# Packing the last 96 gate and up columns of two chunks: one shared full-width tile per chunk and two column tiles

## The chip, the cores and the metric

The kernel runs on one core of a Trainium2 chip. The metric is the device time of one execution in microseconds, median over several runs. Nearly all runs are fast, with a granted TensorE clock of 0.999 to 1.000. PE is TensorE, PEld its weight loads, ACT ScalarE, DVE VectorE, POOL GpSimd.

## The reference, cut to what matters

The input `x` has 2048 rows of 512. It is layer normalised, and the result `xn` feeds a complex diagonal recurrence (with an input and an output projection) and a gated feed-forward block. The output is the sum of both and `x`.

```python
def _B_ref(x, w_gate, w_up, w_down):       # S, D, F = 2048, 512, 1376
    g = _silu(x @ w_gate)
    u = x @ w_up
    return (g * u) @ w_down

xn = _layernorm(x, axis=-1)
return x + _A_ref(xn, ...) + _B_ref(xn, B_w_gate, B_w_up, B_w_down)
```

What matters is that 1376 = 10 x 128 + 96: the gate and up matrices have ten full tiles of 128 columns and one of 96.

## The kernel before

The rows are worked in four chunks of 512. A chunk's transposed, normalised rows are `xnT[:, c % 2]`, so two chunks are on the chip at a time. A gate or up tile is four matmuls (512 input features in four steps) that stream 512 rows each into one PSUM bank. Tiles go in pairs, a pair of banks at a time, and the kernel takes four pairs of banks in turn; ScalarE evicts a pair, and VectorE multiplies gate and up. The eleventh tile stands alone.

```python
FP = [(0, 2), (2, 2), (4, 2), (6, 2), (8, 2), (10, 1)]      # (first tile, number of tiles)

def ffn_mm(c, i, which, bk):
    fs = fsz[i]                                              # 128, or 96 for the last tile
    ...
        for kt in range(KT):                                 # KT = 4
            inst = e.matmul(pbank[0:fs, bk, :]..., lhsT=w[:, kt, i * 128:i * 128 + fs], rhs=xnT[:, c % 2, :, kt, :],
                            start=(kt == 0), stop=(kt == KT - 1))

def ffn_up(c, ip):
    i0, n = FP[ip]
    bk = next_pair()
    for k in range(n):
        ffn_mm(c, i0 + k, "u", bk + k)
    rows = slice(0, 128 if n == 2 else fsz[i0])
    ...
    g.add("act", ... activation(out=uf[rows, ul, 0:n, :]..., in_=pair_f32(rows, bk, 512 * n), func=AF.Identity) ...)
    g.add("dve", ... tensor_tensor(out=hT[rows, hb, i0:i0 + n, :], in0=sg[rows, sl, 0:n, :], in1=uf[rows, ul, 0:n, :], op=ALU.mult) ...)
```

`ffn_gate` is the same with Silu. The order of the stages, which is the order of PE's queue:

```python
for ip in range(3, 6): ffn_gate(0, ip)
for ip in range(3, 6): ffn_up(0, ip)
u0 = ssm_b_chunk(0)                    # input projection of the recurrence
...
ln_chunk(2); xt_chunk_dma(2)           # layer norm of chunk 2, its transpose by DMA
...
u1 = ssm_b_chunk(1)
for ip in range(6): ffn_gate(1, ip); ffn_up(1, ip)
u2 = ssm_b_chunk(2)
...
dc_chunk(0)                            # down and output matrices of chunk 0
...
```

The queues of ScalarE, VectorE and GpSimd are ordered by a list scheduler with estimated durations; PE and the main DMA queue keep the order in which the program names the work.

Of the kernel before, what the change touches and what calls it, by code (L numbers as in the profile page):

```python
# [10 lines left out]
ALU = alu_op_type.AluOpType  # L11
F32 = mybir.dt.float32
B16 = mybir.dt.bfloat16
I32 = mybir.dt.int32
AF = mybir.ActivationFunctionType
# [223 lines left out]
def bass_parallel_sum__ssm_conv_s5__swiglu_ffn__prompt_kernel(  # L239
# [17 lines left out]
    Fh = B_w_gate.shape[1]  # L257
# [5 lines left out]
    KT = D // 128  # L263
    PT = P // 128
    FT = (Fh + 127) // 128
    fsz = [min(128, Fh - i * 128) for i in range(FT)]
# [3 lines left out]
    g = _Graph()  # L270
    es = ExitStack()
    with es:
        block = es.enter_context(nc.Block())

        def sb(name, shape, dt):
            return es.enter_context(nc.sbuf_tensor(name, shape, dt))
# [8 lines left out]
        NXN = 12  # L285
        xn_sb = sb("xn_sb", [128, NXN, D], B16)
        xnT = sb("xnT", [128, 2, 4, KT, 128], B16)
        wg = sb("wg", [128, KT, Fh], B16)
        wu = sb("wu", [128, KT, Fh], B16)
        wd = sb("wd", [128, FT, D], B16)  # L290
        BT = sb("BT", [128, 2, KT, P], B16)
# [1 line left out]
        hT = sb("hT", [128, 2, FT, CH], B16)  # L293
# [32 lines left out]
        NG = 4  # L326
        sg = sb("sg", [128, NG, 2, CH], B16)
        NUF = 2
        uf = sb("uf", [128, NUF, 2, CH], B16)
# [8 lines left out]
        pbank = _PB()  # L338
# [10 lines left out]
        def _bank_live(b):  # L349
            lw = g.last_w.get(("bk", b, 0))  # L350
            rd = g.readers.get(("bk", b, 0), ())
            return lw is not None and lw.eng == "pe" and len(rd) == 0 and not lw.name.startswith("pe_warm")

        def next_pair():
            for _ in range(NB // 2):
                b = 2 * (pair_ctr[0] % (NB // 2))
                pair_ctr[0] += 1
                if not (b in reserved or _bank_live(b) or _bank_live(b + 1)):
                    return b
            raise AssertionError("all PSUM pairs live")  # L360

        def pair_f32(rows, b, n=1024):
            return pb16[rows, b:b + 2, :].rearrange("p a f -> p (a f)").bitcast(F32)[:, 0:n]

        def BK(b):
            return [("bk", b, 0), ("bk", b, 1)]
# [55 lines left out]
        def loads_stage_b2():  # L422
# [12 lines left out]
              reads=[("ones",)], writes=[("ident",)], name="ident", est=300)  # L435
        g.add("pool", lambda e: e.iota(iot[:], pattern=[[1, TP]], base=0, channel_multiplier=0, allow_small_or_imprecise_dtypes=True),
              writes=[("iot",)], name="iota", est=1000)
# [4 lines left out]
              name="act_warm", est=220, order=(act_q[-1],))  # L442
# [22 lines left out]
        def bn_st(a, order=()):  # L465
            return g.add("dve", lambda e, a=a: e.bn_stats(out=st[:, a, :], in_=x_sb[:, a, :]),  # L466
                         reads=[("x", a)], writes=[("st", a)], name="bnst%d" % a, est=640, order=order)

        def bn_ag(a, order=()):
            return g.add("dve", lambda e, a=a: e.bn_aggr(out=mv[:, a, :], in_=st[:, a, :]),  # L470
                         reads=[("st", a)], writes=[("mv", a)], name="bnag%d" % a, est=90, order=order)

        def ln_ve(a, n, eng="dve", order=()):
            return g.add(eng, lambda e: e.tensor_scalar(out=ve[:, a:a + n], in0=mv[:, a:a + n, 1], scalar1=EPS, scalar2=None, op0=ALU.add),  # L474
                         reads=[("mv", a + j) for j in range(n)], writes=[("ve", a + j) for j in range(n)], name="ve%d" % a, est=70 if eng == "dve" else 230, order=order)

        def ln_rstd(a, n):
            return g.add("pool", lambda e: e.tensor_tensor(out=rstd[:, a:a + n], in0=ve[:, a:a + n], in1=mhalf[:, a:a + n], op=ALU.pow),  # L478
                         reads=[("ve", a + j) for j in range(n)] + [("mhalf",)], writes=[("rstd", a + j) for j in range(n)], name="rstd%d" % a, est=370 + 190 * n)
# [11 lines left out]
        def ln_apply_act(a0):  # L491
            g.add("dve", lambda e, a0=a0: e.scalar_tensor_tensor(out=nmr[:, a0:a0 + 4], in0=mv[:, a0:a0 + 4, 0], scalar=-1.0, in1=rstd[:, a0:a0 + 4], op0=ALU.mult, op1=ALU.mult),  # L492
                  reads=[("mv", a0 + j) for j in range(4)] + [("rstd", a0 + j) for j in range(4)], writes=[("nmr", a0 + j) for j in range(4)], name="nmr%d" % a0, est=70)
            for a in range(a0, a0 + 4):
                g.add("act", lambda e, a=a: e.activation(out=xn_sb[:, a % NXN, :], in_=x_sb[:, a, :], func=AF.Identity, scale=rstd[:, a:a + 1], bias=nmr[:, a:a + 1]),  # L495
                      reads=[("x", a), ("rstd", a), ("nmr", a)], writes=[("xn", a % NXN)], name="xn%d" % a, est=710)
# [22 lines left out]
        def ln_chunk(c):  # L519
            for a in range(4 * c, 4 * c + 4):  # L520
                bn_st(a)
                bn_ag(a)
            ln_ve(4 * c, 4, eng="pool")
            ln_rstd(4 * c, 4)
            if _CFG["ln_norm_act"][c]:
                ln_apply_act(4 * c)
            else:
                for a in range(4 * c, 4 * c + 4):
                    ln_apply(a)
# [23 lines left out]
        def xt_chunk_dma(c):  # L553
            s0 = (4 * c) % NXN
            dma("xTd%d" % c, xnT[:, c % 2].rearrange("p j k t -> p (j k) t"), xn_sb[:, s0:s0 + 4, :],
                [("xnT", c % 2, j) for j in range(4)], 4 * TILEB, reads=[("xn", s0 + j) for j in range(4)], xpose=True, prio=_CFG["prio_xt"])
# [136 lines left out]
        gctr = [0]  # L693
        uctr_f = [0]
# [4 lines left out]
                return [("wg", "a0"), ("wg", "a1")]  # L699
            return [(nm, 0 if i < 6 else 1)]  # L700

        FP = [(0, 2), (2, 2), (4, 2), (6, 2), (8, 2), (10, 1)]

        def ffn_mm(c, i, which, bk):
            fs = fsz[i]
# [9 lines left out]

        def silu_pair(c, ip, bk):
            i0, n = FP[ip]
            rows = slice(0, 128 if n == 2 else fsz[i0])
            sl = gctr[0] % NG
            gctr[0] += 1  # L720
            sg_slot[(c, ip)] = sl
            g.add("act", lambda e: e.activation(out=sg[rows, sl, 0:n, :].rearrange("p a t -> p (a t)"), in_=pair_f32(rows, bk, 512 * n), func=AF.Silu),  # L722
                  reads=sum([BK(bk + k) for k in range(n)], []), writes=[("sg", sl)], name="silu%d_%d" % (c, ip), est=63 + 427 * n)

        def ffn_gate(c, ip):
# [3 lines that stand above are left out]
                ffn_mm(c, i0 + k, "g", bk + k)  # L729
            silu_pair(c, ip, bk)  # L730
# [27 lines left out]
        def ffn_up(c, ip):  # L758
            i0, n = FP[ip]
            hb = c % 2  # L760
            bk = next_pair()
            for k in range(n):
                ffn_mm(c, i0 + k, "u", bk + k)
            rows = slice(0, 128 if n == 2 else fsz[i0])
            ul = uctr_f[0] % NUF
            uctr_f[0] += 1
            sl = sg_slot[(c, ip)]
            g.add("act", lambda e: e.activation(out=uf[rows, ul, 0:n, :].rearrange("p a t -> p (a t)"), in_=pair_f32(rows, bk, 512 * n), func=AF.Identity),  # L768
                  reads=sum([BK(bk + k) for k in range(n)], []), writes=[("uf", ul)], name="uev%d_%d" % (c, ip), est=63 + 427 * n)
            g.add("dve", lambda e: e.tensor_tensor(out=hT[rows, hb, i0:i0 + n, :], in0=sg[rows, sl, 0:n, :], in1=uf[rows, ul, 0:n, :], op=ALU.mult),  # L770
                  reads=[("sg", sl), ("uf", ul)], writes=[("hT", hb, i0 + k) for k in range(n)], name="hmul%d_%d" % (c, ip), est=77 + 267 * n)

        usctr = [0]
        uctr = [0]
# [17 lines left out]
        def ssm_b_chunk(c):  # L792
            return [ssm_b_unit(c, pt) for pt in range(PT)]
# [100 lines left out]
        loads_stage_b2()  # L894
        for ip in range(0, 3):
            ffn_up(0, ip)
        for ip in range(3, 6):
            ffn_gate(0, ip)
        for ip in range(3, 6):
            ffn_up(0, ip)  # L900
        u0 = ssm_b_chunk(0)
        ssm_elem_chunk(0, u0)
        ln_chunk(2)
        xt_chunk_dma(2)
        for pt in range(PT):
            wprep_C(pt)
        u1 = ssm_b_chunk(1)
        for ip in range(6):
            ffn_gate(1, ip)
            ffn_up(1, ip)  # L910
        u2 = ssm_b_chunk(2)
# [3 lines left out]
        resid_chunk(1)  # L915
        ln_chunk(3)
        xt_chunk_dma(3)
        for ip in range(6):
            ffn_gate(2, ip)
            ffn_up(2, ip)  # L920
        u3 = ssm_b_chunk(3)
        dc_chunk(1)
        ssm_elem_chunk(2, u2)
        ssm_elem_chunk(3, u3)
        for ip in range(6):
            ffn_gate(3, ip)
            ffn_up(3, ip)
        resid_chunk(2)
# [63 lines left out]
```

## Time and profile before

| | before |
|---|---|
| time, median of the first six runs | 181.66 us (181.49 to 182.05) |
| span of the profiled run | 180.3 us |
| PE, DVE, ACT busy | 97%, 89%, 47% |
| unbroken run of matmuls, from 13.63 us to 177.80 us | 164.17 us |
| the eleventh tiles | 32 matmuls |

First the busy line of the page, then pieces of the chain of waits (start, length, what).

```profile
PE 175.3 (97%) x900; PEld 84.9 (47%) x908; DVE 160.8 (89%) x274; ACT 84.5 (47%) x107; POOL 13.5 (7%) x23
```

```profile
13.63 13.81 PE pb L710 x64
27.44 13.81 PE pb L781 x64
41.26 18.99 PE pb L710 x88
60.25 6.91 PE pb L781 x32
...
175.01 2.79 PE pb L876 x20
```

L710 is the gate/up line, L781 the input projection of the recurrence, L876 the output matrices. From 13.63 us on the chain is PE work end to end. 64 matmuls take 13.81 us, and the 88 of one chunk's gate and up tiles 18.99 us: 215.8 ns each. I call 216 ns a slot. The groups by form (operation, tiles, weight shape, moving shape, count, then busy us, mean ns, and idle time before) show the eleventh tile on each engine:

```profile
L710 PE MATMUL pb<-xnT,wg 128*96 128x512 bf16 x16 | 4.1, 379 | 0.0
L710 PE MATMUL pb<-xnT,wu 128*96 128x512 bf16 x16 | 4.1, 379 | 0.0
L768 ACT ACTIVATE uf<-pb 96x512 bf16<-96x512 f32 x4 | 2.4, 590 | 0.4 <-DVE rot L812 0.4
L722 ACT ACTIVATE sg<-pb 96x512 bf16<-96x512 f32 x4 | 2.3, 586 | 0.0
L770 DVE TENSOR_TENSOR hT<-sg,uf 96x512 bf16<-96x512 bf16 x4 | 1.7, 413 | 0.0
```

A narrow tile is not cheaper: in the timeline of PE the two 96-wide tiles of chunk 1 begin 0.87 us apart, which is four slots.

```profile
58.36 1.03 PE L710 MATMUL pb<-xnT,wg 128*96 128x512 bf16 x4
59.23 1.03 PE L710 MATMUL pb<-xnT,wu 128*96 128x512 bf16 x4
```

The 379 ns are the recorded duration of one matmul, with a modelled end; the next starts 216 ns after it and overlaps the remaining 163 ns. What counts is start to start.

### The profile page before, as it was taken

The numbers are of one execution on the slowest core, as the hardware profiler recorded it, in microseconds if no ns is written. First come the engines' busy times: TensorE is split into PE (matmuls) and PEld (weight loads), VectorE is DVE, ScalarE is ACT, GpSimd is POOL, SyncE is SP. The second block draws the span as 40 slices with busy tenths as digits, with TensorE's granted clock in tenths as the row PEclk, the third lists the DMA queues.
The fourth block names the chain that finished last, engine by engine and source line by source line (L and its number), as shares of the span: only waits on it lengthen the run. The fifth ranks groups of instructions, "written<-read, shape, count | busy, mean of one in ns | idle before, by whom it ended". The sixth has DMA issues, their size and how long they took to land.

```text
span 180.3 us, 2342 instructions
## 1 busy us (share of the span) xinstructions
PE 175.3 (97%) x900; PEld 84.9 (47%) x908; DVE 160.8 (89%) x274; ACT 84.5 (47%) x107; POOL 13.5 (7%) x23
## 2 busy tenths in 40 slices
PE   8799999999999999999999999999999999999994
PEld 2494444444444444444444544444444444444643
DVE  3888849989799999979999999999999999999733
ACT  3279899995897991060655653000455620000000
POOL 3251200004200000320000000000000000000000
PEclk9999999999999999999999999999999999999999
DMA  6995556669160000001430000001200000000202
GB/s 163 316 373 127 119 100 104 149 201 343 33 116 0 4 0 0 0 0 61 91 86 0 0 0 4 0 0 36 80 0 4 0 0 0 0 0 33 87 29 87
DMA packets 23410, 12.37 MB, mean 69 GB/s; under 512 B 15112, under 2 KB 23400, under 8 KB 23400
## 3 DMA queue, kind: packets, MB, share of 16 engines
q1 hardware_dynamic: 22832, 11.70, 24.4%
q10 hardware_dynamic: 568, 0.53, 1.0%
q8 instruction: 7, 0.11, 0.3%
q14 instruction: 3, 0.02, 0.0%
HBM read 6.46 MB, written 2.10 MB: 47 GB/s over the span
## 4 chain that ended last, share of the span: by engine, by line
PE 94%; DMA 1%; DVE 1%; issue 1%; ACT 1%; POOL 0%
PE pb L710 39%; PE pb L863 21%; PE pb L781 15%; PE pb L876 15%; PE pb L749 3%; DMA x_sb<-in_A_x_dram 1%; ACT xnT L549 1%; PE pb L543 1%; DVE st L466 0%; POOL rstd L478 0%; DVE x_sb L881 0%; DVE xn_sb L485 0%; DVE mv L470 0%; DVE ve L474 0%; PE pb L457 0%
## 5 line engine op out<-in xcount | busy, mean ns | idle before, releaser
L710 PE MATMUL pb<-xnT,wu 128*128 128x512 bf16 (+1 forms) x176 | 41.2, 379 | 0.0
L821 DVE TENSOR_TENSOR_SCAN rot<-sm,car,rot 128x512 bf16<-128x512 f32 x32 | 38.9, 1267 | 0.0
L863 PE MATMUL pb<-wd,hT 128*128 128x512 bf16 (+3 forms) x183 | 38.0, 366 | 0.2
L710 PE MATMUL pb<-xnT,wg 128*128 128x512 bf16 (+1 forms) x152 | 35.9, 379 | 0.0
L722 ACT ACTIVATE sg<-pb 128x1024 bf16<-128x1024 f32 (+1 forms) x24 | 22.4, 948 | 28.4 <-PE pb L710 28.1
L876 PE MATMUL pb<-W,hss 128*128 128x512 bf16 (+1 forms) x132 | 28.1, 366 | 0.2
L781 PE MATMUL pb<-xnT,BT 128*128 128x512 bf16 x128 | 28.1, 379 | 0.0
L863 PEld LDWEIGHTS pb<-wd,hT 128*128 128x128 bf16 (+1 forms) x187 | 18.3, 98 | 20.0
L768 ACT ACTIVATE uf<-pb 128x1024 bf16<-128x1024 f32 (+1 forms) x24 | 22.7, 950 | 9.4 <-PE pb L710 8.6
L710 PEld LDWEIGHTS pb<-xnT,wu 128*128 128x128 bf16 (+1 forms) x176 | 17.6, 100 | 20.1
L710 PEld LDWEIGHTS pb<-xnT,wg 128*128 128x128 bf16 (+1 forms) x152 | 15.3, 100 | 17.6
L876 PEld LDWEIGHTS pb<-W,hss 128*128 128x128 bf16 x136 | 13.3, 98 | 14.4
L781 PEld LDWEIGHTS pb<-xnT,BT 128*128 128x128 bf16 x128 | 12.5, 98 | 15.0
L788 ACT ACTIVATE u_sb<-pb 128x1024 bf16<-128x1024 f32 x16 | 16.3, 1022 | 5.1 <-PE pb L781 4.8
L770 DVE TENSOR_TENSOR hT<-sg,uf 128x1024 bf16<-128x1024 bf16 (+1 forms) x24 | 14.9, 635 | 2.8 <-ACT uf L768 2.8
L881 DVE TENSOR_TENSOR x_sb<-pb,x_sb 128x512 bf16<-128x512 f32 (+1 forms) x17 | 10.9, 654 | 5.4 <-PE pb L876 5.4
L466 DVE BATCH_NORM_STATS2 st<-x_sb 128x6 f32<-128x512 bf16 x16 | 10.2, 682 | 4.0 <-DMA x_sb<-in_A_x_dram 4.0
L495 ACT ACTIVATE xn_sb<-x_sb,nmr,rstd 128x512 bf16<-128x512 bf16 x8 | 5.9, 802 | 10.5 <-DVE nmr L492 10.5
L812 DVE TENSOR_TENSOR rot<-u_sb,cosT 128x2048 bf16<-128x2048 bf16 x8 | 9.7, 1215 | 0.4 <-ACT u_sb L788 0.4
L812 DVE TENSOR_TENSOR rot<-rot,sin 128x2048 bf16<-128x2048 bf16 x8 | 9.8, 1220 | 0.0
L812 DVE TENSOR_TENSOR rot<-rot,cosT 128x2048 bf16<-128x2048 bf16 x8 | 9.8, 1220 | 0.0
L812 DVE TENSOR_TENSOR rot<-u_sb,sin 128x2048 bf16<-128x2048 bf16 x8 | 9.7, 1214 | 0.0
(62 smaller groups left out, 115.7 us busy)
## 6 DMA issues: line engine op xcount, KB each, us to landing
out_dram<-x_sb SPq DMA_DIRECT2D x15, 128.0 KB, 1.7
x_sb<-in_A_x_dram SPq DMA_DIRECT2D x3, 512.0 KB, 7.6
wd<-in_B_w_down_dram SPq DMA_DIRECT2D x1, 1280.0 KB, 7.0
wu<-in_B_w_up_dram SPq DMA_DIRECT2D x1, 768.0 KB, 6.4
wg<-in_B_w_gate_dram SPq DMA_DIRECT2D x1, 608.0 KB, 7.5
wu<-in_B_w_up_dram SPq DMA_DIRECT2D x1, 608.0 KB, 8.7
x_sb<-in_A_x_dram SPq DMA_DIRECT2D x4, 128.0 KB, 2.8
wg<-in_B_w_gate_dram ACTq DMA_DIRECT2D x2, 256.0 KB, 4.0
```

The lines of the kernel that those rows point to most:

```text
L466: return g.add("dve", lambda e, a=a: e.bn_stats(out=st[:, a, :], in_=x_sb[:, a, :]), reads=[("x", a)], writes=[("st", a)], name="bnst%d" % ...
L710: inst = e.matmul(pbank[0:fs, bk, :].rearrange("p (j t) -> p j t", j=4), lhsT=w[:, kt, i * 128:i * 128 + fs], rhs=xnT[:, c % 2, :, kt, :], ...
L722: g.add("act", lambda e: e.activation(out=sg[rows, sl, 0:n, :].rearrange("p a t -> p (a t)"), in_=pair_f32(rows, bk, 512 * n), func=AF.Sil ...
L768: g.add("act", lambda e: e.activation(out=uf[rows, ul, 0:n, :].rearrange("p a t -> p (a t)"), in_=pair_f32(rows, bk, 512 * n), func=AF.Ide ...
L770: g.add("dve", lambda e: e.tensor_tensor(out=hT[rows, hb, i0:i0 + n, :], in0=sg[rows, sl, 0:n, :], in1=uf[rows, ul, 0:n, :], op=ALU.mult), ...
L781: inst = e.matmul(pbank[:, bk, :].rearrange("p (j t) -> p j t", j=4), lhsT=BT[:, ri, kt, pt * 128:(pt + 1) * 128], rhs=xnT[:, c % 2, :, kt ...
L788: g.add("act", lambda e: e.activation(out=u_sb[:, us].rearrange("p r t -> p (r t)"), in_=pair_f32(slice(0, 128), b0), func=AF.Identity), r ...
L812: tt = lambda out, a, b, op, r, w, nm: g.add("dve", lambda e: e.tensor_tensor(out=out, in0=a, in1=b, op=op), reads=r, writes=w, name="%s_% ...
L821: g.add("dve", lambda e, A0=A0, A1=A1, k=k, ri=ri, pt=pt: e.tensor_tensor_scan(out=A1[:, k, ri, :], data0=rr[:, pt:pt + 1].to_broadcast([1 ...
L863: inst = e.matmul(pbank[:, bk, 0:nc_], lhsT=hT[0:fs, hb, i, lt * 128:(lt + 1) * 128], rhs=wd[0:fs, i, c0:c0 + nc_], start=(i == 0), stop=F ...
L876: inst = e.matmul(pbank[:, bk, 0:nc_], lhsT=hss[:, hb, pt, ri, lt * 128:(lt + 1) * 128], rhs=W12[:, ri, pt, c0:c0 + nc_], start=False, sto ...
L881: g.add("dve", lambda e, bk=bk, a=a, c0=c0, nc_=nc_: e.tensor_tensor(out=x_sb[:, a, c0:c0 + nc_], in0=pbank[:, bk, 0:nc_], in1=x_sb[:, a, ...
```

## The change

Intent: 96 gate and 96 up columns of two chunks are 384 columns, three full tiles, where the kernel used four. Each chunk gets one 128-wide tile with its 96 gate columns and 32 of its up columns (GpSimd copies those 32 weight columns behind the gate weights). The other 64 up columns share one PSUM bank: chunk `c` on the first 64-column tile of the array, chunk `c + 1` on the second. If the two column tiles run at the same time, 16 slots become 12. The work of a chunk pair moves to where both chunks are on the chip.

```diff
-        FP = [(0, 2), (2, 2), (4, 2), (6, 2), (8, 2), (10, 1)]
+        FP = [(0, 2), (2, 2), (4, 2), (6, 2), (8, 2)]
+        NG0, NU0 = fsz[FL], 2 * fsz[FL] - 128                          # 96, 64
+        g.add("pool", ... tensor_copy(out=wg[:, :, Fh:FT * 128], in_=wu[:, :, FL * 128 + NU0:Fh]) ...)
...
+        def ffn_left(c):
+            bk = next_pair()
+            for k in range(2):
+                def mmg(e, k=k):
+                    for kt in range(KT):
+                        inst = e.matmul(pbank[:, bk + k, :]..., lhsT=wg[:, kt, FL * 128:FT * 128], rhs=xnT[:, (c + k) % 2, :, kt, :], ...)
+            bu = next_pair()
+            def mmu(e):
+                for kt in range(KT):
+                    for k in range(2):
+                        inst = e.matmul(pbank[64 * k:64 * k + NU0, bu, :]..., lhsT=wu[:, kt, FL * 128:FL * 128 + NU0],
+                                        rhs=xnT[:, (c + k) % 2, :, kt, :], start=(kt == 0), stop=(kt == KT - 1))
+            # ACT: Silu of 96 rows x 1024; copy of 32 rows x 1024; copies of 64 rows x 512, twice
+            # DVE: one multiply of 96 x 1024 into hT of both chunks
...
         u0 = ssm_b_chunk(0)
         ssm_elem_chunk(0, u0)
         ln_chunk(2)
+        u1 = ssm_b_chunk(1)
+        ffn_left(0)
         xt_chunk_dma(2)
...
         ssm_elem_chunk(3, u3)
-        for ip in range(6):
+        ffn_left(2)
+        for ip in range(5):
             ffn_gate(3, ip)
```

Two column tiles and two full tiles together are called a group below; there are two groups. Each full matmul has an array tile of 128 x 128 and each 64-wide one a tile of 128 x 64, at column 0 or 64; passing from one to the other is called a change of tiling mode.

More of the change, by code (lines that the diff above doesn't have):

```diff
@@ L287, in bass_parallel_sum__ssm_conv_s5__swiglu_ffn__prompt_kernel @@
         xnT = sb("xnT", [128, 2, 4, KT, 128], B16)
-        wg = sb("wg", [128, KT, Fh], B16)
+        wg = sb("wg", [128, KT, FT * 128], B16)
         wu = sb("wu", [128, KT, Fh], B16)
@@ L700, in wres @@
             return [(nm, 0 if i < 6 else 1)]
-        FP = [(0, 2), (2, 2), (4, 2), (6, 2), (8, 2), (10, 1)]
+        FP = [(0, 2), (2, 2), (4, 2), (6, 2), (8, 2)]
+        FL = FT - 1
+        NG0, NU0 = fsz[FL], 2 * fsz[FL] - 128
+        g.add("pool", lambda e: e.tensor_copy(out=wg[:, :, Fh:FT * 128], in_=wu[:, :, FL * 128 + NU0:Fh]), reads=[("wu", 1)], writes=[("wg", 2)], name="wgx", est=300)
         def ffn_mm(c, i, which, bk):
@@ L717, in silu_pair @@
             i0, n = FP[ip]
-            rows = slice(0, 128 if n == 2 else fsz[i0])
+            rows = slice(0, 128)
             sl = gctr[0] % NG
@@ L763, in ffn_up @@
                 ffn_mm(c, i0 + k, "u", bk + k)
-            rows = slice(0, 128 if n == 2 else fsz[i0])
+            rows = slice(0, 128)
             ul = uctr_f[0] % NUF
@@ L771, in ffn_up @@
                   reads=[("sg", sl), ("uf", ul)], writes=[("hT", hb, i0 + k) for k in range(n)], name="hmul%d_%d" % (c, ip), est=77 + 267 * n)
+        def ffn_left(c):
[3 more added lines that the diff above has]
+                    for kt in range(KT):
+                        inst = e.matmul(pbank[:, bk + k, :].rearrange("p (j t) -> p j t", j=4), lhsT=wg[:, kt, FL * 128:FT * 128], rhs=xnT[:, (c + k) % 2, :, kt, :],
+                                        start=(kt == 0), stop=(kt == KT - 1))
+                    return inst
+                g.add("pe", mmg, reads=[("wg", 1), ("wg", 2)] + [("xnT", (c + k) % 2, j) for j in range(4)],
+                      writes=BK(bk + k), name="mm_g%d_%d" % (c + k, FL), est=4 * 216, ninst=4)
+            bu = next_pair()
+            def mmu(e):
+                for kt in range(KT):
+                    for k in range(2):
+                        inst = e.matmul(pbank[64 * k:64 * k + NU0, bu, :].rearrange("p (j t) -> p j t", j=4), lhsT=wu[:, kt, FL * 128:FL * 128 + NU0],
+                                        rhs=xnT[:, (c + k) % 2, :, kt, :], start=(kt == 0), stop=(kt == KT - 1))
+                return inst
+            g.add("pe", mmu, reads=[("wu", 1)] + [("xnT", (c + k) % 2, j) for k in range(2) for j in range(4)],
+                  writes=BK(bu), name="mm_ul%d" % c, est=5 * 216, ninst=8)
+            sl = gctr[0] % NG
+            gctr[0] += 1
+            ul = uctr_f[0] % NUF
+            uctr_f[0] += 1
+            g.add("act", lambda e: e.activation(out=sg[0:NG0, sl].rearrange("p a t -> p (a t)"), in_=pair_f32(slice(0, NG0), bk), func=AF.Silu),
+                  reads=BK(bk) + BK(bk + 1), writes=[("sg", sl)], name="silul%d" % c, est=917)
+            g.add("act", lambda e: e.activation(out=uf[NU0:NG0, ul].rearrange("p a t -> p (a t)"), in_=pair_f32(slice(NG0, 128), bk), func=AF.Identity),
+                  reads=BK(bk) + BK(bk + 1), writes=[("uf", ul)], name="uevx%d" % c, est=917)
+            for k in range(2):
+                g.add("act", lambda e, k=k: e.activation(out=uf[0:NU0, ul, k, :], in_=pbank[64 * k:64 * k + NU0, bu, :], func=AF.Identity),
+                      reads=BK(bu), writes=[("uf", ul)], name="uevl%d_%d" % (c, k), est=490)
+            g.add("dve", lambda e: e.tensor_tensor(out=hT[0:NG0, :, FL, :], in0=sg[0:NG0, sl], in1=uf[0:NG0, ul], op=ALU.mult),
+                  reads=[("sg", sl), ("uf", ul)], writes=[("hT", k, FL) for k in range(2)], name="hmull%d" % c, est=611)
@@ L896, in bass_parallel_sum__ssm_conv_s5__swiglu_ffn__prompt_kernel @@
             ffn_up(0, ip)
-        for ip in range(3, 6):
+        for ip in range(3, 5):
             ffn_gate(0, ip)
-        for ip in range(3, 6):
+        for ip in range(3, 5):
             ffn_up(0, ip)
@@ L906, in bass_parallel_sum__ssm_conv_s5__swiglu_ffn__prompt_kernel @@
             wprep_C(pt)
-        u1 = ssm_b_chunk(1)
-        for ip in range(6):
+        for ip in range(5):
             ffn_gate(1, ip)
@@ L917, in bass_parallel_sum__ssm_conv_s5__swiglu_ffn__prompt_kernel @@
         xt_chunk_dma(3)
-        for ip in range(6):
+        for ip in range(5):
             ffn_gate(2, ip)
@@ L924, in bass_parallel_sum__ssm_conv_s5__swiglu_ffn__prompt_kernel @@
         ssm_elem_chunk(3, u3)
-        for ip in range(6):
+        ffn_left(2)
+        for ip in range(5):
             ffn_gate(3, ip)
```

## The prediction

> **What bounds the kernel now.** TensorE. The chain of waits is 94% PE; from 13.63 to 177.8 us it is one run of matmuls with a few 0.05 us pieces between. In the groups view the gate/up matmuls have an idle time of 0.0 us. In the chain 64 matmuls of 512 columns take 13.81 us and 88 take 18.99 us: 215.8 ns each at a granted clock of 1.0, also with 96-wide weights. DVE is 89% busy, but about 1% of the chain. So matmul slots of 216 ns count.
>
> **What the change does to PE.** The eleventh gate/up tile (96 of 128 columns) costs 2 x 4 matmuls per chunk, 32 in all (groups by form: 16 + 16 with 96-wide weights) = 6.91 us. After: 16 full matmuls (96 gate and 32 up columns) = 3.45 us, and 16 of 64 columns in two column tiles. If the two of a pair run side by side, they take 8 slots = 1.73 us, and 1.73 us are saved. [...] My estimate of a drain is a matmul's recorded 379 ns less its 216 ns pace, 0.16 us; two per group, two groups: 0.65 us. (Weight loads, 98 ns at 128 wide, 123 ns at 96 wide, are hidden; I expect the same of most 64-wide ones.) Net saving about 1.1 us: 1.7 at best, 0 or a loss of 0.3 if the tiles run one after the other.
>
> **What it moves.** ACT: eight evictions of 96x512 at 0.59 us (4.7 us) become, per group, two of 1024 columns at 1.02 us and two of 512 at 0.59 us: 6.4 us. ACT is 47% busy, but about 89% from 27 to 41 us, just before the first group. Three other PSUM pairs of 1.73 us stand between a late eviction and PE, so I expect no PE wait. DVE: four multiplies at 0.41 us become two at 0.68 us. POOL gets one small copy. Until the first group everything comes 1.7 us earlier: the first state projection at 25.7 us (its weights land at 23.7 us), the second at 32.6 us (its transposed chunk lands near 28 us). The third chunk's transpose is issued at 49.6 us, takes 4.2 us and is needed at 59.5 us. The last recurrence results are written by 165.9 us and wanted at 170.9 us now, at about 169.7 us after: 3.9 us of slack. No wait should swallow the gain.
>
> **On the critical path:** all of the PE saving, one for one; none of the ACT, DVE or POOL changes.
>
> **Predicted:** 180.5 us (0.6% less), range 179.7 to 181.8. Faster by over 2%: 0.01. Within 2%: 0.97. Slower by over 2%: 0.02.
>
> **What would show it.** The PE timeline of a group: 8 full matmuls at 216 ns, a gap of 0.1 to 0.2 us, then eight 64-wide matmuls, a pair per 216 ns or a little over; the group 2.6 to 3.0 us against 3.45 us. Groups view: idle before gate/up and state matmuls still near 0.0 us. Chain still over 93% PE.
>
> **What would make it wrong.** Column tiles that don't overlap (about 181.7 us); weight loads that stand open between the pairs [...]; a new order on DVE or ACT, whose queues the changed graph reorders, making PE wait after the first group.

1.73 us saved less 0.65 us for four changes of tiling mode is 1.08 us, the "about 1.1 us". "Drain" is the prediction's word for PE time lost at such a change. Its size was the author's estimate, 379 - 216 ns from the trace of the kernel before.

## The result, and the profile after

| | before | changed |
|---|---|---|
| time, median of six runs | 181.66 us | 180.66 us (180.38 to 181.22) |
| ratio of fast runs | | 0.9946, 95% interval 0.9926 to 0.9966 |
| span of the profiled run | 180.3 us | 178.8 us |
| unbroken run of matmuls | 164.17 us | 163.10 us (13.22 to 176.32 us) |
| PE, DVE, ACT busy | 97%, 89%, 47% | 98%, 90%, 48% |

A ratio is the mean time of one kernel's fast runs over that of the other's of the same rounds, so it is not quite the ratio of the medians quoted. By the 2% rule the change is "same"; the interval says that it is about half a per cent faster.

The chain of waits of the changed kernel's first profile, with the pieces that answer to those of before (L713 is now the gate/up line, L818 the input projection, L781 a group's full tiles, L791 its column tiles, L913 the output matrices):

```profile
13.22 12.09 PE pb L713 x56
25.30 13.81 PE pb L818 x64
39.12 1.73 PE pb L781 x8
40.84 0.98 PE pb L791 x8
41.83 8.74 PE pb L713 x40
50.57 0.04 issue
50.60 8.81 PE pb L713 x40
59.41 6.91 PE pb L818 x32
...
123.33 1.73 PE pb L781 x8
125.06 0.98 PE pb L791 x8
126.04 17.37 PE pb L713 x80
...
169.38 6.94 PE pb L913 x40
```

Eight tiled matmuls take 0.98 us, not the 1.73 us of eight slots. The groups by form:

```profile
L781 PE MATMUL pb<-xnT,wg 128*128 128x512 bf16 x16 | 3.8, 379 | 0.0
L791 PE MATMUL pb<-xnT,wu 128*64 128x512 bf16 x16 | 2.1, 385 | 0.0
L791 PEld LDWEIGHTS pb<-xnT,wu 128*64 128x64 bf16 x16 | 0.7, 109 | 1.3 <-ACT sm L604 0.4 <-issue 0.4
L800 ACT ACTIVATE sg<-pb 96x1024 bf16<-96x1024 f32 x2 | 2.0, 1019 | 17.4 <-PE pb L781 17.4
L802 ACT ACTIVATE uf<-pb 32x1024 bf16<-32x1024 f32 x2 | 2.0, 1016 | 0.0
L805 ACT ACTIVATE uf<-pb 64x512 bf16<-64x512 f32 x4 | 2.4, 592 | 0.2
L807 DVE TENSOR_TENSOR hT<-sg,uf 96x1024 bf16<-96x1024 bf16 x2 | 1.4, 679 | 0.0
```

ACT's evictions of the two groups are 2.0 + 2.0 + 2.4 = 6.4 us where the eleventh tiles took 4.7 us, and DVE's multiplies 1.4 us where they took 1.7 us, as costed. The 64-wide weight loads are no faster than wide ones (109 ns against 98 ns).

The start times of single matmuls in the trace's records show the mechanism (first group, times in us; "full" is 128 wide):

```
40.249 full   40.465 full
40.774 tile   40.778 tile      309 ns after the last full one
41.014 tile   41.018 tile      240 ns after the first tile
41.230 tile   41.234 tile      216
41.447 tile   41.449 tile      217
41.761 full                    314
41.987 full                    226
42.204 full                    217
```

The two tiles of a pair start 2 to 4 ns apart, and a pair takes one slot (216 and 217 ns to the third and fourth pair). From 40.465 to 42.204 us there are seven steps; seven slots would be 1.51 us, and it takes 1.74 us. So a group pays 0.23 us around its tiled part: 0.093 us going in, 0.024 us at the second pair, 0.098 us going out and 0.010 us after that. The records put the first 64-wide weight load 1 ns before its matmul, so the 0.093 us lie before that load and not in it. The sum for the kernel is then: eight slots saved (1.73 us) less 2 x 0.23 us = 1.27 us.

The run of matmuls shrank by only 1.07 us in this profile. The other 0.2 us are in the chain at 50.57 us: five blocks of eight matmuls from 41.83 us took 8.74 us, the next block was due at 50.41 us (the one before began at 48.68 us) and began at 50.60 us. The ACT timeline shows what stood ahead of the eviction that it waited for:

```profile
44.21 1.02 ACT L725 ACTIVATE sg<-pb 128x1024 bf16<-128x1024 f32 x1
46.71 2.93 ACT L495 ACTIVATE xn_sb<-x_sb,nmr,rstd 128x512 bf16<-128x512 bf16 x4 [1.47 <-DVE nmr L492]
49.55 1.00 ACT L771 ACTIVATE uf<-pb 128x1024 bf16<-128x1024 f32 x1
```

The up pair that L771 evicts was computed by about 45.3 us, but its eviction stands behind the four layer norm instructions of chunk 2, and those wait for statistics of rows that land late: VectorE sat idle for 1.19 us until the DMA of the rows had landed, and began the statistics at 40.98 us. The eviction ends at 50.55 us, and PE goes on 0.05 us later. The span shrank by more than the run of matmuls only because this profile's run began 0.41 us sooner; that start lies between 13.06 and 13.87 us over the profiles of kernels whose first stage is the same, so it is scatter and no gain.

### The profile page after: what moved, and what is told of

The parts are those of the page before. It is cut to its first block, busy times and chain, and to the rows that moved or that the text cites. A ratio compares the mean times of both kernels' runs of the same rounds, so it can differ in the third digit from the quotient of the medians.

```text
span 178.8 us, 2346 instructions
## 1 busy us (share of the span) xinstructions
PE 174.5 (98%) x908; PEld 82.9 (46%) x908; DVE 160.6 (90%) x272; ACT 86.5 (48%) x107; POOL 13.0 (7%) x24
## 4 chain that ended last, share of the span: by engine, by line
PE 95%; DMA 2%; ACTq 1%; ACT 0%; DVE 0%; issue 0%
PE pb L713 36%; PE pb L900 21%; PE pb L913 15%; PE pb L818 15%; PE pb L752 3%; DMA wg<-in_B_w_gate_dram 2%; PE pb L781 2%; PE pb L791 1%; ACTq L385 1%; PE pb L543 0%; ACT xnT L549 0%; DVE x_sb L918 0%; PE pb L457 0%
## 5 line engine op out<-in xcount | busy, mean ns | idle before, releaser
L900 PE MATMUL pb<-wd,hT 128*128 128x512 bf16 (+3 forms) x187 | 38.7, 367 | 0.0
L713 PE MATMUL pb<-xnT,wu 128*128 128x512 bf16 x160 | 37.3, 379 | 0.0
L713 PE MATMUL pb<-xnT,wg 128*128 128x512 bf16 x136 | 32.0, 380 | 0.0
L913 PE MATMUL pb<-W,hss 128*128 128x512 bf16 (+1 forms) x136 | 28.3, 367 | 0.0
L818 PE MATMUL pb<-xnT,BT 128*128 128x512 bf16 x128 | 28.1, 379 | 0.0
L725 ACT ACTIVATE sg<-pb 128x1024 bf16<-128x1024 f32 x20 | 20.2, 1021 | 10.5 <-PE pb L713 10.2
L713 PEld LDWEIGHTS pb<-xnT,wu 128*128 128x128 bf16 x160 | 15.5, 98 | 18.9 <-ACT uf L771 0.5
L771 ACT ACTIVATE uf<-pb 128x1024 bf16<-128x1024 f32 x20 | 20.4, 1021 | 7.1 <-PE pb L713 5.7
L713 PEld LDWEIGHTS pb<-xnT,wg 128*128 128x128 bf16 x136 | 13.1, 98 | 16.4 <-issue 0.8
L913 PEld LDWEIGHTS pb<-W,hss 128*128 128x128 bf16 x136 | 13.3, 98 | 14.4
L818 PEld LDWEIGHTS pb<-xnT,BT 128*128 128x128 bf16 x128 | 12.5, 98 | 15.1
L773 DVE TENSOR_TENSOR hT<-sg,uf 128x1024 bf16<-128x1024 bf16 x20 | 13.4, 677 | 2.1 <-ACT uf L771 2.1
L800 ACT ACTIVATE sg<-pb 96x1024 bf16<-96x1024 f32 x2 | 2.0, 1019 | 17.4 <-PE pb L781 17.4
```

What stands on the lines that cost most here:

```text
L713: inst = e.matmul(pbank[0:fs, bk, :].rearrange("p (j t) -> p j t", j=4), lhsT=w[:, kt, i * 128:i * 128 + fs], rhs=xnT[:, c % 2, :, kt, :], ...
L725: g.add("act", lambda e: e.activation(out=sg[rows, sl, 0:n, :].rearrange("p a t -> p (a t)"), in_=pair_f32(rows, bk, 512 * n), func=AF.Sil ...
L771: g.add("act", lambda e: e.activation(out=uf[rows, ul, 0:n, :].rearrange("p a t -> p (a t)"), in_=pair_f32(rows, bk, 512 * n), func=AF.Ide ...
L773: g.add("dve", lambda e: e.tensor_tensor(out=hT[rows, hb, i0:i0 + n, :], in0=sg[rows, sl, 0:n, :], in1=uf[rows, ul, 0:n, :], op=ALU.mult), ...
L818: inst = e.matmul(pbank[:, bk, :].rearrange("p (j t) -> p j t", j=4), lhsT=BT[:, ri, kt, pt * 128:(pt + 1) * 128], rhs=xnT[:, c % 2, :, kt ...
L900: inst = e.matmul(pbank[:, bk, 0:nc_], lhsT=hT[0:fs, hb, i, lt * 128:(lt + 1) * 128], rhs=wd[0:fs, i, c0:c0 + nc_], start=(i == 0), stop=F ...
```

## The experiments

The best yardstick is the unbroken run of matmuls, because it leaves the scatter of the start out. It is read from the chain: from the first piece of the gate/up line that is over 8 us long to the end of the last PE piece before the final VectorE addition.

| kernel | run of matmuls, us | against before | time, us | before, same runs | ratio (95%) |
|---|---|---|---|---|---|
| before | 164.17 | | 181.66 | | |
| changed, first profile | 163.10 | -1.07 | 180.66 | 181.66 | 0.9946 (0.9926 to 0.9966) |
| e0 changed again | 162.90 | -1.27 | 180.57 | 181.77 | 0.9934 (0.9919 to 0.9949) |
| e1 tiles in turn | 162.93 | -1.24 | 180.48 | 181.77 | 0.9927 (0.9911 to 0.9944) |
| e2 moved, unpacked | 164.17 | 0.00 | 181.75 | 181.87 | 0.9997 (0.9979 to 1.0014) |
| e3 eviction first | 162.91 | -1.26 | 180.70 | 181.77 | 0.9937 (0.9921 to 0.9953) |
| e4 twice the changes | 163.36 | -0.81 | 181.39 | 181.77 | 0.9971 (0.9954 to 0.9988) |
| e5 second group only | 163.54 | -0.63 | 180.94 | 181.87 | 0.9952 (0.9934 to 0.9970) |
| e6 one tile, two banks | 164.62 | +0.45 | 182.07 | 181.87 | 1.0013 (0.9993 to 1.0033) |
| e11 rows first | 162.90 | -1.27 | 180.44 | 181.64 | 0.9939 (0.9925 to 0.9952) |

My theory was that the gain is the side-by-side run of the two column tiles, less a fixed price at each change of tiling mode. Rivals were that it comes from the moved work and its new queue orders, or that 64-wide matmuls are cheap by themselves; and, for the missing 0.2 us, that the wait was a late eviction, chance, or a price of the mode change.

### e0: the changed kernel again

No edit.

> The changed kernel unaltered, as the yardstick of this batch. Both theories: 180.7 us, ratio to before 0.994 to 0.996; the PE clock of work the same as in its first profile: a group's eight tiled matmuls 0.98 us, the wait of about 0.2 us near 50.4 us again. If that wait is chance, it is not there in this profile.

The chain of this profile:

```profile
41.19 0.98 PE pb L791 x8
42.17 17.37 PE pb L713 x80
```

The group costs the same, but the wait is not there: 80 matmuls take 17.37 us, which is 80 slots (17.27 us as in chunk 2) and the 0.1 us of the change back to full width. Here the layer norm began at 45.97 us, not at 46.71 us, and the eviction behind it at 48.80 us:

```profile
44.62 1.02 ACT L725 ACTIVATE sg<-pb 128x1024 bf16<-128x1024 f32 x1
45.97 2.93 ACT L495 ACTIVATE xn_sb<-x_sb,nmr,rstd 128x512 bf16<-128x512 bf16 x4 [0.32 <-POOL rstd L478]
48.80 1.00 ACT L771 ACTIVATE uf<-pb 128x1024 bf16<-128x1024 f32 x1
```

So the wait comes and goes from run to run. The PE saving of 1.27 us does not. The wait follows the start of the layer norm, counted from the start of the run of matmuls: at 32.41 us (e0) and 33.19 us (e1) there is none, at 33.49 us (first profile) it is 0.20 us, at 33.93 us (e7) 0.61 us.

### e1: the same tiles in turn, not in alternation

```diff
-                for kt in range(KT):
-                    for k in range(2):
+                for k in range(2):
+                    for kt in range(KT):
```

> The same sixteen 64-wide matmuls, but four on one column tile and then four on the other instead of in alternation; all engine queues are otherwise the same. Theory (the gain is the side-by-side run of neighbours in the queue): only the last of the first tile and the first of the second can start together, so a group takes 7 slots of 216 ns in place of 4: +0.65 us a group, +1.3 us in all, about 181.9 us, slower than before. Rival (the array finds the free tile by itself, whatever the order): same time as the changed kernel, pairs still 4 ns apart. Rival (the gain is the changed order, not the tiles): same time as the changed kernel.

My theory of alternation was wrong: nothing changed. In the records the pairs start 13 ns apart in place of 4 ns, and the second pair follows 240 ns after the first as before. The compiled program does have the four matmuls of the first tile ahead of the four of the second (e1, e7 and e8: all three keep the order of the kernel). A rival, that the array finds the free tile whatever the order, had to be shown directly (e7).

### e6: both chunks on the same column tile

```diff
-  inst = e.matmul(pbank[64 * k:64 * k + NU0, bu, :]..., lhsT=wu[:, kt, FL * 128:FL * 128 + NU0], ...)
+  inst = e.matmul(pbank[0:NU0, bu + k, :]..., lhsT=wu[:, kt, FL * 128:FL * 128 + NU0], ...)
```

The evictions follow the outputs; the engines' queues keep their order.

> The same sixteen 64-wide matmuls, both chunks on the first column tile and into two PSUM banks, no second tile. Theory (two tiles run at the same time): with one tile a group takes 8 slots of 216 ns in place of 4: 0.86 us more a group, 1.7 us in all, about 182.3 us, about 0.4 us slower than before. Rival (64-wide matmuls or this placement are simply cheap, which the run with the tiles in turn did not rule out): 180.6 us, still four slots a group.

The chain:

```profile
40.92 1.84 PE pb L791 x8
42.76 17.37 PE pb L713 x80
```

Eight slots are 1.73 us, and it takes 1.84 us, with 0.1 us more behind it: the mode change is still paid, and the second tile is what made the difference. The packed kernel without parallel tiles is 0.45 us longer on PE than the kernel before, which is 2 x 0.23 us. In time it is not told from the kernel before (1.0013, 0.9993 to 1.0033). The narrow matmul alone gains nothing; side by side the eight are 1.84 / 0.98 = 1.9 times as fast.

### e7: telling the two tiles apart

```diff
+  for kt in range(KT):                                        # first tile: four of 512 columns
+      e.matmul(pbank[0:NU0, bu, :]..., rhs=xnT[:, c % 2, :, kt, :], ...)
+  for kt in range(KT):                                        # then second tile: eight of 256 columns
+      for h in range(2):
+          e.matmul(pbank[64:64 + NU0, bu, h * 256:(h + 1) * 256]..., rhs=xnT[:, (c + 1) % 2, 2 * h:2 * h + 2, kt, :], ...)
```

> Tiles in turn again, but the second tile's work, queued behind all of the first tile's, is cut into matmuls of 256 columns, so that the trace tells the tiles apart. Theory after the run with the tiles in turn (a matmul whose tile is free starts ahead of earlier ones that wait for another tile): the first 256-column matmul starts within some tens of ns of the first 512-column one, and the two kinds stay interleaved to the end; group still about 1.0 us. Rival (matmuls start strictly in the order of the queue): all 512-column ones start before the first of 256 columns, group about 1.5 us.

The PE timeline (L790 is the first tile, L794 the second, queued behind all of L790):

```profile
40.68 0.40 PE L790 MATMUL pb<-xnT,wu 128*64 128x512 bf16 x1
40.70 0.41 PE L794 MATMUL pb<-xnT,wu 128*64 128x256 bf16 x2
40.92 0.38 PE L790 MATMUL pb<-xnT,wu 128*64 128x512 bf16 x1
40.94 0.38 PE L794 MATMUL pb<-xnT,wu 128*64 128x256 bf16 x2
...
41.69 0.39 PE L713 MATMUL pb<-xnT,wg 128*128 128x512 bf16 x1
```

The second tile's first matmul starts at 40.70 us, ahead of three matmuls that stand before it in the queue. So here a matmul of the other column tile starts out of its order, 0.02 us after the first one of the first tile (40.68 us). This profile also had the wait near 50 us, behind a layer norm that began at 47.05 us, and a longer one: two matmul starts there are 0.83 us apart in place of 0.22 us, so PE lost 0.61 us.

### e8: how far ahead

```diff
-                for kt in range(KT):
-                    for k in range(2):
+                for k in range(2):
+                    for rep in range(16):
+                        for kt in range(KT):
```

The sums are made sixteen times over; the result stays right and the time is meant to grow.

> How far ahead the array looks: each group's tiled work is done sixteen times over (the same sums again, right result), 64 matmuls on the first tile and then 64 on the second. If all later work is seen: 64 slots of 216 ns, 13.8 us a group, the two tiles in pairs from the start. If matmuls only start ahead from a window of W matmuls, the second tile begins when the first has 64 - W done, and the group takes (128 - W) slots; with no looking ahead beyond the four seen so far about 124 slots, 26.8 us. The slot at which pairs begin gives W. Total 25 to 52 us longer than the changed kernel.

```profile
39.29 1.73 PE pb L781 x8
41.02 26.91 PE pb L792 x128
```

128 matmuls take 26.91 us, which is 124.7 slots, of which about half a slot is the change of mode (an estimate from the 0.093 and 0.024 us of the first profile). In the records the matmuls stand singly 216 ns apart for 60 starts, then come four pairs, then sixty single ones. The records don't name the tile, but with 64 and 64 queued in turn this must be the last four of the first tile beside the first four of the second. So the second tile began beside the 61st matmul of the first, ahead of three that stand before it in the queue with their weight loads, and no sooner. What sets that limit, matmuls, loads or both, is not shown. In e1 each tile had just four, and the group's eight took 0.99 us in turn against 0.98 us in alternation; with 64 in turn only four pairs ran side by side.

### e4: the mode changes twice as often

```diff
+            for h in range(2):
+                g.add("pe", lambda e, h=h: mmg(e, h), ...)                      # full tile of chunk c + h
+                g.add("pe", lambda e, h=h: mmu(e, (2 * h, 2 * h + 1)), ...)     # half of the column tiles
```

> The tiled matmuls of a group cut in two blocks of four with a full-width block between, so eight mode changes in place of four, same number of matmuls. Theory (a change costs about 0.1 us in the open, whichever way, beside 216 ns a pair): PE time of a group grows by 0.2 us, the total by 0.4 us, to about 181.1 us. Rival (the 0.22 us over four pair slots is a cost per tiled matmul or per weight load): no growth, 180.7 us.

The run of matmuls is 163.36 us, 0.46 us longer than in e0, for four more changes: 0.11 us each, as in the records above. The time of 181.39 us is 0.8 us above e0's, more than that; in the profiled runs 0.31 us of the difference are a later start (13.87 us against 13.56 us), which is within the scatter of the start. The starts of the runs without a profile are not known. A few operations of DVE and ACT also moved in their queues, but PE waited for none of them. The theory of a fixed price per change stands.

### e2: moved but not packed

```diff
+        def ffn_left(c):                      # in the kernel before
+            for k in range(2):
+                ffn_gate(c + k, 5)
+                ffn_up(c + k, 5)
```

and the stages in the order of the change.

> The kernel before with the eleventh tiles moved to where the change puts them (chunks 0 and 1 after the second state projection, chunks 2 and 3 after the second output stage), but not packed: 32 full-width slots. Theory (the gain is the packing): no gain, 181.6 us, ratio to before 0.998 to 1.002. Rival (the gain comes from moving work out of the first 26 us or from the new queue orders): 180.6 us.

The run of matmuls is 164.17 us to the hundredth as before, the time ratio 0.9997. The move alone gives nothing.

### e5: the second group only

Chunks 0 and 1 with the stages and tiles of before, chunks 2 and 3 packed.

> The change for chunks 2 and 3 alone; chunks 0 and 1 as before. Theory (each group gives the same on PE): half of the saving, 0.65 us off the span, about 181.1 us, ratio about 0.9965. Rival (the gain is all in the first group, where the early stages come sooner): 181.7 us.

The run of matmuls is 0.63 us shorter, half of 1.27 us. The time fell by 0.93 us by the medians, more than half, but this profile's run also began early, at 13.06 us; the interval of the ratio (0.9934 to 0.9970) holds the expected 0.9965.

### e3: the eviction ahead of the layer norm

```diff
         streams = _schedule(g.tasks, engs)
+        sa = streams["act"]
+        ev = next(t for t in sa if t.name == "uev1_0")
+        sa.remove(ev)
+        sa.insert(min(k for k, t in enumerate(sa) if t.name in ("xn8", "xn9", "xn10", "xn11")), ev)
```

> Only one thing moved in the changed kernel: in ScalarE's queue the eviction of the first up pair of chunk 1 stands ahead of the four layer norm instructions of chunk 2, not behind them. Theory (PE waited near 50.4 us because a PSUM pair was released late by ScalarE, which had sat idle before the layer norm): the 0.2 us wait of PE and the idle time of 1.5 us on ScalarE before the layer norm are gone, span 0.2 us shorter, time about 180.45 us. Rival (the wait comes from the mode change or from VectorE's late multiplies): the wait stays, time 180.65 us.

No gain in time or in the run of matmuls: 180.70 us. It was inconclusive, because the yardstick (e0) had no wait to take away. The eviction did move, from 48.80 us in e0 to 45.78 us. To settle the cause of the wait, it had to be made larger.

### e9 and e10: the rows of chunk 2 later, without and with that order

```diff
+        ss = streams["sp"]
+        lx = next(t for t in ss if t.name == "ld_x8")
+        ss.remove(lx)
+        ss.insert(1 + next(k for k, t in enumerate(ss) if t.name == "ld_wd0"), lx)
```

This only puts the load of the rows of chunk 2 behind the load of the down weights; e10 has also the edit of e3.

> The changed kernel, but the load of the input rows of chunk 2 is issued after the large load of the down weights, so it lands some 3 to 4 us later; all compute queues stay as they were. Theory (the 0.2 us wait of PE seen in the first profile is a late eviction, queued on ScalarE behind the layer norm of chunk 2, which waits for these rows): the layer norm starts at about 49 to 50 us, the eviction behind it near 53 us, and PE, which wants that PSUM pair at about 50.5 us, waits 2.5 to 3.5 us; time about 183 to 184 us. Rival (the wait has another cause, such as the mode change or the PSUM pairs of the group): PE waits no more than before, 180.6 us, since the rows are needed late.

> As the run with the late rows, with one ScalarE instruction moved: the eviction of the first up pair of chunk 1 ahead of the layer norm. Theory: that eviction is done by about 46.8 us whatever the rows do; the next PSUM pair to run out is then wanted one step of 1.73 us later, so PE waits about 1.7 us less than in the run beside it: about 181.3 to 182.3 us. Rival: both alike.

The ACT queue of e9 and then the PE timeline of e9 and of e10:

```profile
50.12 2.93 ACT L495 ACTIVATE xn_sb<-x_sb,nmr,rstd 128x512 bf16<-128x512 bf16 x4 [4.69 <-DVE nmr L492]
52.96 1.00 ACT L771 ACTIVATE uf<-pb 128x1024 bf16<-128x1024 f32 x1
```

```profile
48.82 1.89 PE L713 MATMUL pb<-xnT,wg 128*128 128x512 bf16 x8
54.02 1.90 PE L713 MATMUL pb<-xnT,wu 128*128 128x512 bf16 x8 [3.31 <-ACT uf L771]
```

```profile
50.74 1.89 PE L713 MATMUL pb<-xnT,wu 128*128 128x512 bf16 x8
54.53 1.90 PE L713 MATMUL pb<-xnT,wg 128*128 128x512 bf16 x8 [1.91 <-ACT sg L725]
```

With late rows the layer norm begins at 50.12 us, and the eviction behind it releases PE after 3.31 us of idle time. With that one eviction moved ahead, PE gets one block further, and the idle time is 1.91 us, 1.4 us less (expected about 1.7 us; the rows also landed half a microsecond later in e10, at 44.9 us against 44.4 us). In e9 as in the first profile and in e7, PE goes on 0.05 to 0.06 us after the end of the eviction by L771; in e10 it goes on 0.05 us after the end of the eviction by L725. The time of e10 is 182.62 us (ratio 1.0080, 1.0021 to 1.0139), against 181.65 us of before and 181.3 to 182.3 us expected. The four runs of e9 are 183.94 us (the profiled one), 185.81, 186.40 and 187.15 us, the last in the slow state; the ratio of the three fast ones is 1.0208 (1.0144 to 1.0272), unclear by the 2% rule. The profiled run fits the expected 183 to 184 us; why the others were longer, at granted clocks of 0.982 to 0.991, stays open, so only the traces are used here. So the cause of the wait is settled: an eviction that stands in ScalarE's queue behind a layer norm that waits for a DMA.

### e11: an attempt at a better version

```diff
         def loads_stage_b2():
+            dma("ld_x8", x_sb[:, 8:12, :], x_v[:, 8:12, :], ...)
             dma("ld_cre", CT[:, 0], A_C_re, ..., xpose=True)
             dma("ld_cim", CT[:, 1], A_C_im, ..., xpose=True)
-            dma("ld_x8", x_sb[:, 8:12, :], x_v[:, 8:12, :], ...)
```

> An attempt at a better version: the changed kernel with the load of the input rows of chunk 2 issued ahead of the two transposed loads of the output matrix, so it lands some 8 us earlier; the queues are scheduled anew, and the layer norm instructions of chunk 2 now stand singly between evictions. Theory (now and then PE loses about 0.2 us to an eviction behind a late layer norm): no PE wait near 50 us in any profile, run of matmuls 162.9 us, time 180.4 to 180.6 us, at best 0.1 us below the changed kernel on average. Rival (the margin is enough as it is, or the cosine tables that now come later cost more): the same or slower than the changed kernel.

The layer norm of chunk 2 now begins at 36.99 us, its instructions stand singly between evictions, and PE has no wait near 50 us. The run of matmuls is 162.90 us, the best value of e0. The time of 180.44 us (180.41 to 180.70 in five runs) has a ratio to before of 0.9939, no different from the changed kernel's 0.9934 and 0.9946. It takes the risk away; that it is faster on average is not shown.

## Why the prediction was right, point by point

- **PE bounds, slots count.** Right. The change of the run of matmuls in every experiment that kept the tiled work and had no wait is the number of slots times 216 ns and the mode changes, within 0.03 us (with 0.115 us a change, from the first profile): -1.73 + 4 x 0.115 = -1.27 (e0: -1.27); with eight changes -0.81 (e4: -0.81); one group -0.63 (e5: -0.63); no saved slot and four changes +0.46 (e6: +0.45).
- **The two column tiles overlap.** Right: 4 ns apart, a pair per slot, 0.98 us for eight; and shown to be the second tile and nothing else by e6.
- **The drain.** Right that each change of tiling mode costs PE time, size too large. The prediction estimated "0.16 us; two per group, two groups: 0.65 us". Measured are 0.11 to 0.12 us, 0.46 us in all. The estimate took the part of a matmul's recorded duration that overlaps the next one as fully exposed. e4 shows that the cost goes with the number of changes, and e6 that it needs no second tile. What the array does at a change, and so whether it is a drain, no run shows.
- **Weight loads.** Right. A 64-wide load takes 109 ns, a 128-wide one 98 ns; why, no run shows. Between the later pairs the loads are hidden, since the third and fourth pair follow after 216 and 217 ns. The cause of the 0.024 us more at the second pair is not shown.
- **"No wait should swallow the gain."** Wrong in part. The prediction looked at ACT's busy share and at the three PSUM pairs in reserve (5.2 us), but not at the order in ACT's queue. The eviction could start about 4.2 us after its data were ready (45.3 to 49.55 us), and took another 1.0 us, so the reserve was used up. The first profile of the changed kernel lost 0.2 us there and its second (e0) nothing; e7, whose tiled matmuls are cut otherwise, lost 0.6 us. In the first profile the two errors, 0.19 us too much for the mode changes and 0.2 us of unforeseen wait, nearly cancel, which is luck.
- **The total.** Predicted 180.5 us, a gain of about 1.1 us; measured 180.66 us in the first runs and 180.57 us in the second, gains of 1.00 and 1.20 us.
- **Everything earlier until the first group.** Right in its mechanism: the first state projection began at 25.30 us, and its weights were there. No gain comes from it (e2).
- **The last recurrence results.** Written by 164.78 us and wanted at 169.38 us: 4.6 us of slack, where 3.9 us were expected.

## What to carry to other kernels

Two 64-column tiles with different moving data ran side by side here: with outputs at partitions 0 to 63 and 64 to 127 of PSUM eight matmuls took 0.98 us, with both at 0 to 63, in two banks, 1.84 us (e6). Keep the matmuls of the two close in the queue: four of each in turn still overlapped (e1), of 64 in turn only four pairs did (e8). And collect them in one block, because each entry to and each exit from the tiled mode cost 0.11 to 0.12 us here, about half a slot. Count what a packing saves in slots of the bounding engine before anything else; here that sum, with the measured price of a change, accounts to within 0.03 us for the run of matmuls of the eight profiles checked that had no wait (e0 to e6 and e11). Before you call an eviction harmless, look at what stands ahead of it in its engine's queue and what that waits for: a share of 47% busy hid an eviction 4 us late.
